# A Fourier mixing layer feeding a GEGLU block: a re-ordered opening, four weight scalings and one fold half moved to GpSimd, and new slots for the third batch's fold

## The chip, the cores and the metric

One core of one Trainium2 chip runs the whole program. The metric is the device time of one execution in microseconds (us); smaller is better. In what follows PE is TensorE, ACT is ScalarE, DVE is VectorE, POOL is GpSimd and SP is SyncE. PE multiplies, ACT and DVE empty PSUM, POOL works from SBUF alone, and SP only issues DMAs. POOL also issues DMAs: those that cast or gather.

## The reference

```
x: (8, 3008, 256) float32                      # batch, sequence, channels
a = real(fft(fft(x, axis=1), axis=2))          # mixing, float32
t = a.reshape(24064, 256)
g, v = t @ w_gate, t @ w_val                   # (256, 1536) each
out = (gelu(g) * v) @ w_out                    # exact gelu; (1536, 256)
```

## The kernel before

**The transform.** Each batch's sequence of 3008 is split as 94 x 32. The kernel first "folds" x: it adds and subtracts mirrored rows and channels, so that half-size transforms are left. `fold_ops` cuts this into five pieces of the 17 columns j: (13,4), (9,4), (5,4), (1,4), (0,1), each being start and count. A piece has a `first` (forward plus mirrored rows, lines 221 and 222) and a `second` (line 225). From batch 1 on there are two `combine` steps besides (line 229). The result is the tile `eo`. `s1` and `s1t` multiply it with the table G (lines 508 and 549), `ch` combines channels (line 530), and `tp_e`, `tp_o` and `tp_y` multiply with the table TP (lines 585, 590, 609). This leaves the even and odd halves E and O of one batch, and the row EB. The channel transform is not carried out on the data. `make_w` multiplies it into the gate and value weights instead (line 448): the table CW times the raw weights `w_raw` gives W for E, W for O, and "M", which is -2 times W for O except in row 0 (`keep2`, lines 463 and 465).

**The FFN.** A batch has three chunks of up to 512 token columns (512, 512, 481), each with twelve blocks of 128 hidden units. One block of one chunk is a **slot**: 36 slots for each batch, 288 in all. In slot i PE does the gate (`l1_gate`, E and O), then the mirrored gate of slot i-1 by adding M times O into the same PSUM bank (`l1_gate2`), then the value of this slot and of the one before. ACT applies gelu twice. DVE multiplies. POOL makes the mirrored half of h (line 732), except in the first eight slots, where the value too has three matmuls (`three`) and DVE does both halves (lines 707 and 724). The second layer (`l2_piece`, line 757) of a chunk runs in the slots of the next chunk.

**What sets the order.** Every engine runs its instructions in the order in which the program issues them; that order is written out by hand. `opening()` issues the loads, the tables and batch 0's transform, ending with E, O and the first 256 columns of W. `feed()` then walks the slots. In slot i it issues gate, gate2 of i-1, value, a piece of layer 2, then `pool[i]`, value2 of i-1, another piece of layer 2, and last `fill[i]`. `plan()` fills the two tables: `fill` holds what remains of the weights, batch 0's chunks 1 and 2, loads and transforms of later batches; `pool` holds the folds of batch b, by the list `slot_of`. The transform `s1t(b, jg, g)` of a piece stands no sooner than two slots after the slot of that piece's last fold step (`ready`). `load_part(b+1, k)` stands one slot after the `second` of the piece that frees its buffer.

**Loads in the opening.** SP loads columns 9 to 16 and 0 of batch 0 (`x_stage`). POOL issues 21 DMAs, in this order: five for batch 0 (`cast_mirror`, `cast_forward`), two each for w_raw columns 0-255, 256-511, 512-1023 and 1024-1535 (gate, then value), six for batch 1, and `load_wo(0)`, `load_wo(1)` for the two halves of w_out. Further down this numbering is used: DMA 10 and 11 are w_raw 512-1023, DMA 12 and 13 are w_raw 1024-1535, DMA 14 and 15 bring the first fold piece of batch 1. On SP, `load_part(2, ...)` brings the forward half of batch 2 into `x_raw`. Its buffer is the one that holds batch 0's `xb[0]`, so it can start when the last fold of batch 0 has read that.

**Warm-up matmuls.** `warm(n)` issues n matmuls of 512 columns on a zero tile; nothing reads their result.

Of the kernel before, what the change touches and what calls it, by code (L numbers as in the profile page):

```python
# [11 lines left out]
AF = mybir.ActivationFunctionType  # L12
ALU = mybir.AluOpType
# [15 lines left out]
def kernel(  # L29
# [8 lines left out]
    nc = tc.nc  # L38
# [8 lines left out]
    NK = 24  # L47
# [216 lines left out]
    def reduced(d, r, f):  # L264
        nc.vector.tensor_scalar(r, f, MAGIC, None, op0=ALU.add)
        nc.vector.scalar_tensor_tensor(d, r, MAGIC, f, op0=ALU.subtract, op1=ALU.subtract)
# [97 lines left out]

    def cw_phases():
        nc.scalar.activation(cf[:, 0:128], row_c, AF.Copy, scale=col_n0)
        reduced(cd[:, 0:128], cr[:, 0:128], cf[:, 0:128])

    def cw_magnitude():
# [22 lines left out]
    def t_columns():  # L392
        ps = psum("v")
        for i in range(5):
            nc.tensor.matmul(ps[:, i : i + 1], par[:, i, :], one[:, int(i == 0) : int(i == 0) + 1], start=True, stop=True)  # L395
        nc.scalar.activation(parc, ps[:, 0:5], AF.Copy)

    def t_phases():
        k1 = _sub(row_t, [[1, K1]], 0)
        for i in range(2):  # L400
            nc.scalar.activation(
                tf[:, i * K1 : (i + 1) * K1], k1, AF.Identity, scale=parc[:, 0:1], bias=parc[:, 1 + i : 2 + i])

    def t_reduced():
        reduced(td[:, :], tr[:, :], tf[:, :])
# [33 lines left out]

    V3_TO = 1024  # L440

    def make_w(i, f0, n, parts=(0, 1), engine="A", m_at=None, tag="dft"):

        def run():
            ps = psum(tag)
            for k, part in enumerate(parts):
                for half in range(2):
                    nc.tensor.matmul(  # L448
                        ps[:, k * n : (k + 1) * n], CW[:, part, half, :], w_raw[:, i, half, f0 : f0 + n],
                        start=half == 0, stop=half == 1)  # L450
            m = n * len(parts)
            dst = _sub(W_sb, [[F, len(parts)], [1, n]], (2 * i + parts[0]) * F + f0)
            if engine == "A":
                nc.scalar.activation(dst, ps[:, :m], AF.Copy)
            else:
                nc.vector.tensor_copy(dst, ps[:, :m])  # L456
            if 1 in parts and (i == 0 or f0 < V3_TO):
                def minus():
                    if i and f0 == 0:
                        W["v", "M"] = work([128, V3_TO], BF16, "osb", 3, "w_minus")[:, :]  # L460
                    dst, src = W["gv"[i], "M"][:, f0 : f0 + n], ps[:, m - n : m]
                    if engine == "A":
                        nc.scalar.activation(dst, src, AF.Copy, scale=keep2)
                    else:
                        nc.vector.tensor_scalar(dst, src, keep2, None, op0=ALU.mult)

                if m_at is None:
                    minus()
                else:
                    m_at.append(minus)  # L470
        return run
# [44 lines left out]
                nc.vector.tensor_copy(dst, src)  # L516
        return run

    def ch(b, pp, engine="A"):

        def run():
            st = state(b)
            A = st["A"]
            if "Z" not in st:
                st["Z"] = Z_tile()
            ps = ps_any(b)
            for q in range(2):
                k = 2 * (2 * pp + q)
                for g in range(2):
                    nc.tensor.matmul(  # L530
                        ps[:, q * C : (q + 1) * C], _sub(A, [[1, 128]], g * NK * K1 + k * K1), II[:, g, :, :],
                        start=g == 0, stop=g == 1)
            dst = _sub(st["Z"], [[1, 512]], pp * 512)
            if engine == "A":
                nc.scalar.activation(dst, ps[:, :], AF.Copy)
            else:
                nc.vector.tensor_copy(dst, ps[:, :])
        return run

    def s1t(b, jg, half):  # L540
# [252 lines left out]
    def opening():  # L793
        stage[0] = stage_tile()
        xb[0] = xb_tile(0)
        for j0, nj, at in ((9, 8, 0), (0, 1, 8)):
            nc.sync.dma_start(
                out=_sub(stage[0], [[1, nj * C]], at * C),
                in_=ap_replace(x, ap=[[32 * C, NPX], [1, nj * C]], offset=x.offset + j0 * C))
        pool_consts()  # L800
        index_consts(0)
        cast_mirror(0, 9, 8)
        pool_consts2()
        cast_mirror(0, 5, 4)
        cast_forward(0, 1, 8)
        index_consts(1)
        cast_mirror(0, 0, 1)
        cast_mirror(0, 1, 4)
        for f0, n in ((0, 256), (256, 256), (512, 512), (1024, 512)):
            load_w(f0, n)  # L810
        xb[1] = xb_tile(1)
        cast_forward(1, 9, 8)
        cast_mirror(1, 9, 8)
        cast_forward(1, 0, 9)
        for j0, nj in ((5, 4), (1, 4), (0, 1)):
            cast_mirror(1, j0, nj)
        for q in range(2):
            load_wo(q)
        idle = gelu_tile()[:, 0, :]
        nc.vector.memset(one[:, 0:1], 1.0)  # L820
        sin_table()
        nc.vector.memset(idle, 0.0)

        def warm(n):

            ps = psum("o")
            for _ in range(n):
                nc.tensor.matmul(ps[:, :], idle[:, 0:128], idle[:, :], start=True, stop=True)  # L828

        def fold_piece(j0, nj):  # L830
            for f in fold_ops(0, j0, nj, nc.vector):
                f()

        vec_consts()
        vec_fills()
        warm(7)
        g_phases()
        t_columns()
        t_phases()
        g_rows(9, 7)  # L840
        t_reduced()
        vec_consts2()
        identities()
        cw_phases()
        g_ends()
        cw_magnitude()
        vec_fills2()
        g_rows(1, 8)
        t_sin()
        cw_sin()  # L850
        gelu_table()
        warm(6)
        fold_piece(9, 4)
        s1(0, 2, 0)()
        s1(0, 2, 1)()
        warm(8)
        fold_piece(13, 4)
        cw_rest()
        fold_piece(5, 4)
        s1(0, 1, 0)()  # L860
        s1(0, 1, 1)()
        warm(2)
        fold_piece(0, 1)
        s1(0, 3, 0)()
        s1(0, 3, 1)()
        fold_piece(1, 4)
        t_write()
        s1(0, 0, 0)()
        s1(0, 0, 1, "V")()
        minus = []  # L870
        make_w(0, 0, 256, m_at=minus, tag="o")()
        ch(0, 0)()
        ch(0, 1, "V")()
        make_w(1, 0, 256, m_at=minus, tag="g")()
        tp_e(0, 0, 0, "V", tag="v")()
        tp_e(0, 0, 1, "A", tag="v")()
        minus[0]()
        minus[1]()

    def behind_first_gate():  # L880
        tp_y(0, 0)()

    NS = NG * NFC

    def plan():
# [8 lines left out]
            e = "A" if gi == 1 else "V"  # L894
            early += [ch(0, 2 * gi), ch(0, 2 * gi + 1, e), tp_e(0, gi), tp_o(0, gi, e), tp_y(0, gi)]
        for s, f in (
                (0, make_w(0, 256, 256)), (0, make_w(1, 256, 256, engine="V")), 
                (1, make_w(1, 512, 512, (1,))), (2, make_w(0, 512, 512, (0,), "V")), 
                (3, make_w(0, 512, 512, (1,))), (3, make_w(1, 512, 512, (0,), "V")),
                (4, make_w(1, 1024, 512, (1,), "V")), (5, make_w(0, 1024, 512, (0,), "V")),   # L900
                (6, make_w(0, 1024, 512, (1,))), (6, make_yw()), (7, make_w(1, 1024, 512, (0,), "V"))):
            at(fill, s, f)
        for i, f in enumerate(early):
# [21 lines left out]
        for b in range(1, B):  # L925
# [2 lines left out]
            for j0, nj in PIECES:  # L928
                ops += fold_ops(b, j0, nj, nc.gpsimd)
            per = len(ops) // 5  # L930
            first, n = {2: (s0 - 10, 27), 3: (s0 - 19, 30)}.get(b, (s0 - 22, 32))
            slot_of = [first + i * n // len(ops) for i in range(len(ops))]
            if b == 1:
                slot_of = [4, 4, 5, 5, 6, 6, 7, 7, 8, 8, 9, 13, 13, 14, 15, 15, 16, 17, 17, 18]
            for s, f in zip(slot_of, ops):
# [24 lines left out]
    def feed():  # L960
# [11 lines left out]
        for i, (parts, fc) in enumerate(blocks):  # L972
            if fc == 0 and i:
                assert not pend
                pend = list(works[i // NFC - 1])
            two = sooner.pop(i, []) if i <= NFC + 2 else [pend.pop(0) for _ in range(2) if pend]
            parts["G"][fc]()
            if i == 0:
                behind_first_gate()
            if before:  # L980
                before[0]["g"][before[1]]()
            parts["V"][fc]()
            if len(two) == 2:
                two.pop(0)()
            for f in pool.pop(i, []):
                f()
            if before:
                before[0]["v"][before[1]]()
            if two:
                two.pop(0)()  # L990
            for f in fill.pop(i, []):
                f()
            before = parts, fc
# [38 lines left out]
```

## Time and profile before

| | us |
|---|---|
| median of 9 runs | 623.9 |
| lowest, highest | 622.69, 625.6 |
| the profiled execution, own time | 623.92 |
| its span in the profile | 621.9 |
| E and O ready, first gate matmul of slot 0 | 20.85 |
| first fold step of batch 1 on POOL | 32.65 |
| first gate matmul of slot 3, of slot 18 | 27.16, 59.38 |
| first gate matmul of slot 36 (batch 1) | 95.46 |
| last matmul group begins | 616.58 |

The profiled execution lies at the median; about 2 us of its time lie outside the span. A slot takes about 2 us from there on. Times in the text are from the span's start. The profile's views used below are: the page of totals; the chain of work that ended last, followed back from the end; the instructions of an engine in order of time, with what ended the idle time before each in square brackets; the list of waits; and the bytes moved by each DMA queue within a stretch. "Landing" is the end of a transfer, counted from its issue.

### The profile page before, as it was taken

The numbers are of one execution on the slowest core, as the hardware profiler recorded it, in microseconds if no ns is written. First come the engines' busy times: TensorE is split into PE (matmuls) and PEld (weight loads), VectorE is DVE, ScalarE is ACT, GpSimd is POOL, SyncE is SP. The second block draws the span as 40 slices with busy tenths as digits, with TensorE's granted clock in tenths as the row PEclk, the third lists the DMA queues.
The fourth block names the chain that finished last, engine by engine and source line by source line (L and its number), as shares of the span: only waits on it lengthen the run. The fifth ranks groups of instructions, "written<-read, shape, count | busy, mean of one in ns | idle before, by whom it ended". The sixth has DMA issues, their size and how long they took to land.

```text
span 621.9 us, 12788 instructions
## 1 busy us (share of the span) xinstructions
PE 612.3 (98%) x4229; PEld 407.3 (66%) x4229; DVE 576.7 (93%) x939; ACT 426.0 (69%) x827; POOL 504.8 (81%) x510
## 2 busy tenths in 40 slices
PE   8999999999999999999999999999999999999997
PEld 3456666666766666666666666666666666666666
DVE  7589998999999999999999999999999999999992
ACT  5878677767776677667766667667676667666661
POOL 8389899999997999879997899979987655555651
PEclk9999999999999999999999999999999999999999
DMA  9961736555463353631644335543122321221123
GB/s 177 233 97 27 206 93 158 113 143 143 121 152 94 103 137 87 179 108 41 170 119 122 106 81 134 137 106 93 49 64 68 93 72 46 66 52 40 42 52 82
DMA packets 52464, 65.40 MB, mean 105 GB/s; under 512 B 7627, under 2 KB 47276, under 8 KB 50002
## 3 DMA queue, kind: packets, MB, share of 16 engines
q1 hardware_dynamic: 45470, 49.03, 30.2%
q0 software_dynamic: 6608, 15.29, 11.5%
q8 instruction: 33, 0.54, 0.4%
q10 hardware_dynamic: 320, 0.26, 0.2%
q14 instruction: 33, 0.27, 0.2%
HBM read 39.65 MB, written 30.17 MB: 112 GB/s over the span
## 4 chain that ended last, share of the span: by engine, by line
PE 91%; POOL 2%; DVE 2%; DMA 2%; issue 2%; ACT 1%; SPq 0%; DVEq 0%; ACTq 0%; POOLq 0%
PE ps_o L757 37%; PE ps_g L668 28%; PE ps_v L668 19%; PE ps_dft L549 2%; PE ps_dft L585 1%; PE ps_o L828 1%; DMA out_dram<-out_sb 1%; POOL h_sb L732 1%; DMA EB_sb<-yrow 1%; POOL eo_sb L229 1%; PE ps_dft L448 0%; SPq L662 0%; PE ps_v L395 0%; ACT gelu_sb L684 0%; POOL ab_sb L222 0%
## 5 line engine op out<-in xcount | busy, mean ns | idle before, releaser
L732 POOL TENSOR_TENSOR h_sb<-gelu_sb,v_sb 128x512 bf16<-128x512 bf16 (+1 forms) x280 | 319.5, 1146 | 88.2 <-DVE v_sb L730 82.8
L757 PE MATMUL ps_o<-Wo_sb,h_sb 128*128 128x256 bf16 (+1 forms) x2232 | 334.5, 273 | 0.6 <-POOL h_sb L732 0.6
L757 PEld LDWEIGHTS <-h_sb 128*128 128x128 bf16 (+1 forms) x2304 | 228.7, 100 | 111.7 <-POOL h_sb L732 1.9
L684 ACT ACTIVATE gelu_sb<-ps_g 128x512 bf16<-128x512 f32 (+1 forms) x288 | 169.5, 589 | 98.7 <-PE ps_g L668 90.6
L712 DVE SCALAR_TENSOR_TENSOR ve_sb<-EB_sb,yw,ps_v 128x512 f32<-128x512 bf16 (+1 forms) x280 | 206.3, 737 | 21.5 <-PE ps_v L668 18.3
L668 PEld LDWEIGHTS <-W_sb 128*128 128x128 bf16 x1440 | 138.0, 98 | 80.8 <-issue 3.2
L728 DVE TENSOR_TENSOR h_sb<-gelu_sb,ps_v 128x512 bf16<-128x512 bf16 (+1 forms) x280 | 189.8, 678 | 1.1 <-ACT gelu_sb L693 0.7
L730 DVE SCALAR_TENSOR_TENSOR v_sb<-ve_sb,ps_v 128x512 f32<-128x512 f32 (+1 forms) x280 | 187.4, 669 | 0.0
L668 PE MATMUL ps_g<-O_sb,W_sb 128*128 128x512 bf16 (+1 forms) x576 | 168.9, 374 | 0.1
L693 ACT ACTIVATE gelu_sb<-ps_g 128x512 bf16<-128x512 f32 (+1 forms) x288 | 168.8, 586 | 0.0
L668 PE MATMUL ps_g<-E_sb,W_sb 128*128 128x512 bf16 (+1 forms) x288 | 108.0, 375 | 0.7 <-ACT gelu_sb L693 0.4
L668 PE MATMUL ps_v<-E_sb,W_sb 128*128 128x512 bf16 (+1 forms) x288 | 108.0, 375 | 0.6 <-DVE W_sb L456 0.5
L668 PE MATMUL ps_v<-O_sb,W_sb 128*128 128x512 bf16 (+1 forms) x288 | 108.0, 375 | 0.0
L777 ACT ACTIVATE out_sb<-ps_o 128x512 f32<-128x512 f32 x92 | 55.0, 598 | 35.0 <-PE ps_o L757 34.7
L229 POOL TENSOR_TENSOR eo_sb<-ab_sb 94x512 bf16<-94x512 f32 (+1 forms) x70 | 77.6, 1110 | 0.5
L552 ACT ACTIVATE S_sb<-ps_dft 96x512 bf16<-96x512 f32 x56 | 33.0, 590 | 19.1 <-PE ps_dft L549 19.1
L225 POOL TENSOR_TENSOR ab_sb<-x_raw,x_raw 94x508 f32<-94x508 f32 (+1 forms) x30 | 33.0, 1100 | 0.0
L222 POOL TENSOR_TENSOR ab_sb<-x_raw,x_raw 94x508 f32<-94x508 f32 (+1 forms) x30 | 32.9, 1098 | 0.0
L549 PE MATMUL ps_dft<-eo_sb,G 94*96 94x256 bf16 x119 | 22.3, 272 | 0.2 <-POOL eo_sb L229 0.2
L595 ACT ACTIVATE E_sb<-ps_dft 128x512 bf16<-128x512 f32 (+1 forms) x23 | 13.5, 588 | 8.7 <-PE ps_dft L585 8.7
L163 POOL DMA_INDIRECT x_raw<-in_x_dram,idx x18 | 17.0, 947 | 2.9 <-issue 1.3
L595 ACT ACTIVATE O_sb<-ps_dft 128x512 bf16<-128x512 f32 (+1 forms) x22 | 13.0, 589 | 7.3 <-PE ps_dft L585 6.7
(151 smaller groups left out, 208.5 us busy)
## 6 DMA issues: line engine op xcount, KB each, us to landing
out_dram<-out_sb SPq DMA_DIRECT2D x364, 64.0 KB
x_raw<-in_x_dram SPq DMA_DIRECT2D x10, 768.0 KB
Z_sb<-z SPq DMA_DIRECT2D x7, 768.0 KB
z<-S_sb SPq DMA_DIRECT2D x7, 576.0 KB
EB_sb<-yrow SPq DMA_DIRECT2D x6, 376.2 KB
z<-S_sb SPq DMA_DIRECT2D x7, 192.0 KB
x_raw<-in_x_dram SPq DMA_DIRECT2D x2, 640.0 KB
x_stage<-in_x_dram SPq DMA_DIRECT2D x1, 768.0 KB
```

Source lines behind the costliest of these rows:

```text
L225: eng.tensor_tensor(ab(1, 1, up), mir(1, up), fwd(255, down), op=ALU.add)
L229: eng.tensor_tensor(_sub(eo, [[C, nj], [1, 128]], j0 * C + g * 128), ab(0, 0, [[1, 128]]), ab(1, 0, [[1, 128]]), op=op)
L549: nc.tensor.matmul(ps[:96, q * C : (q + 1) * C], G[:, j, :], _sub(eo, [[1, C]], j * C), start=(j == js[0]), stop=(j == js[-1]))
L668: nc.tensor.matmul(ps[:, :n], W[nm, part][:, fs], src, start=start, stop=stop, **kw)
L684: nc.scalar.activation(gl[:, 0, :n], pg[:, :n], AF.Gelu)
L693: nc.scalar.activation(_sub(gl, [[-1, n]], TOK + n - 1), pg[:, :n], AF.Gelu)
L712: nc.vector.scalar_tensor_tensor(ve[:, :n], EB_bufs[b][:, c0 : c0 + n], yw[:, fc : fc + 1], pv[:, :n], op0=ALU.mult, op1=ALU.add)
L728: nc.vector.tensor_tensor(st["h"][:, fc, 0, :n], gl[:, 0, :n], pv[:, :n], op=ALU.mult)
L730: nc.vector.scalar_tensor_tensor(_sub(vv, [[-1, n]], n - 1), ve[:, :n], 2.0, pv[:, :n], op0=ALU.mult, op1=ALU.subtract)
L732: nc.gpsimd.tensor_tensor(st["h"][:, fc, 1, :n], gl[:, 1, :n], vv[:, :n], op=ALU.mult)
L757: nc.tensor.matmul(pso[:m, half], st["h"][:, fc, sign, h0 : h0 + m], Wo_sb[:, fc, :], start=(fc == 0 and not (first and sign)), stop=(fc = ...
L777: nc.scalar.activation(_sub(osb, [[1, 2 * C]], 0, part_num=m), pso[:m, :], AF.Copy)
```

## The change

The tables CW and II of the channel step are made while DVE would wait for the TP table's phases; TP's phases are moved behind them, and behind the first fold piece. `warm(7)`, `warm(6)` and `warm(2)` become one `warm(16)` at the start; `warm(8)` stays. The `second` of fold piece (13,4) is issued on POOL, between the loads of w_raw 0-255 and 256-511. `cw_rest` and `t_write` move further down DVE's order. `ch` is cut into quarters that alternate between ACT and DVE. `tp_e(0,0,0)` goes to ACT and `tp_e(0,0,1)` to DVE. Of the "M" weights, the one for the value columns 0-255 goes to DVE, and four go to POOL, which reads W for O from SBUF instead of PSUM. `load_wo(1)` leaves the opening for slot 3. `tp_y(0,0)` leaves slot 0 for slot 5. Batch 2's folds get a list of slots written out by hand; before, the formula gives 26, 27, 28, 30, 31, 32, 34, 35, 36, 38, 39, 40, 42, 43, 44, 46, 47, 48, 50, 51.

```diff
     def make_w(... m_engine=None ...)
-                    if engine == "A":
+                    if m_engine == "P":
+                        nc.gpsimd.tensor_scalar(dst, W["gv"[i], "O"][:, f0 : f0 + n], keep2, None, op0=ALU.mult)
+                    elif (m_engine or engine) == "A":
                         nc.scalar.activation(dst, src, AF.Copy, scale=keep2)
...
     def opening():
...
         cast_mirror(0, 1, 4)
-        for f0, n in ((0, 256), (256, 256), (512, 512), (1024, 512)):
+        load_w(0, 256)
+        pool_second = fold_ops(0, 13, 4, nc.gpsimd)[1]
+        pool_second()
+        for f0, n in ((256, 256), (512, 512), (1024, 512)):
             load_w(f0, n)
...
-        for q in range(2):
-            load_wo(q)
+        load_wo(0)
...
         vec_consts()
         vec_fills()
-        warm(7)
+        warm(16)
         g_phases()
-        t_columns()
-        t_phases()
+        columns = t_columns()
         g_rows(9, 7)
-        t_reduced()
         vec_consts2()
         identities()
+        vec_fills2()
         cw_phases()
+        cw_reduced()
         g_ends()
         cw_magnitude()
-        vec_fills2()
         g_rows(1, 8)
+        t_phases(columns)
+        cw_sin()
+        fold_piece(9, 4)
+        t_reduced()
         t_sin()
-        cw_sin()
         gelu_table()
-        warm(6)
-        fold_piece(9, 4)
         s1(0, 2, 0)()
         s1(0, 2, 1)()
         warm(8)
-        fold_piece(13, 4)
-        cw_rest()
+        fold_ops(0, 13, 4, nc.vector)[0]()
         fold_piece(5, 4)
         s1(0, 1, 0)()
         s1(0, 1, 1)()
-        warm(2)
         fold_piece(0, 1)
         s1(0, 3, 0)()
         s1(0, 3, 1)()
         fold_piece(1, 4)
-        t_write()
         s1(0, 0, 0)()
+        cw_rest()
         s1(0, 0, 1, "V")()
         minus = []
         make_w(0, 0, 256, m_at=minus, tag="o")()
-        ch(0, 0)()
-        ch(0, 1, "V")()
-        make_w(1, 0, 256, m_at=minus, tag="g")()
-        tp_e(0, 0, 0, "V", tag="v")()
-        tp_e(0, 0, 1, "A", tag="v")()
+        ch(0, 0, qs=(0,))()
+        t_write()
+        ch(0, 0, "V", qs=(1,))()
+        ch(0, 1, qs=(0,))()
+        ch(0, 1, "V", qs=(1,))()
+        make_w(1, 0, 256, m_at=minus, m_engine="V", tag="g")()
+        tp_e(0, 0, 0, "A", tag="v")()
+        tp_e(0, 0, 1, "V", tag="v")()
         minus[0]()
         minus[1]()
...
     def plan():
...
-                (0, make_w(0, 256, 256)), (0, make_w(1, 256, 256, engine="V")), 
-                (1, make_w(1, 512, 512, (1,))), (2, make_w(0, 512, 512, (0,), "V")), 
-                (3, make_w(0, 512, 512, (1,))), (3, make_w(1, 512, 512, (0,), "V")),
-                (4, make_w(1, 1024, 512, (1,), "V")), (5, make_w(0, 1024, 512, (0,), "V")), 
+                (0, make_w(0, 256, 256, m_engine="P")), (0, make_w(1, 256, 256, engine="V", m_engine="P")),
+                (1, make_w(1, 512, 512, (1,), m_engine="P")), (2, make_w(0, 512, 512, (0,), "V")),
+                (3, make_w(0, 512, 512, (1,), m_engine="P")), (3, lambda: load_wo(1)), (3, make_w(1, 512, 512, (0,), "V")),
+                (4, make_w(1, 1024, 512, (1,), "V")), (5, make_w(0, 1024, 512, (0,), "V")), (5, tp_y(0, 0)),
...
-            first, n = {2: (s0 - 10, 27), 3: (s0 - 19, 30)}.get(b, (s0 - 22, 32))
+            first, n = (s0 - 19, 30) if b == 3 else (s0 - 22, 32)
             slot_of = [first + i * n // len(ops) for i in range(len(ops))]
+            if b == 2:
+                slot_of = [26, 27, 28, 29, 30, 31, 32, 33, 37, 38, 39, 40, 42, 43, 44, 45, 49, 49, 50, 51]
...
     def feed():
...
             parts["G"][fc]()
-            if i == 0:
-                behind_first_gate()
```

`ch(b, pp, engine, qs)` evacuates only the halves q in `qs`, into the same place of Z. `t_columns` now returns its PSUM tile, and `t_phases` copies it out; `cw_reduced` is the DVE half of `cw_phases`.

More of the change, by code (lines that the diff above doesn't have):

```diff
@@ L366, in cw_phases, with cw_reduced @@
         nc.scalar.activation(cf[:, 0:128], row_c, AF.Copy, scale=col_n0)
+    def cw_reduced():
         reduced(cd[:, 0:128], cr[:, 0:128], cf[:, 0:128])
@@ L395, in t_columns, with t_phases @@
             nc.tensor.matmul(ps[:, i : i + 1], par[:, i, :], one[:, int(i == 0) : int(i == 0) + 1], start=True, stop=True)
+        return ps
+    def t_phases(ps):
         nc.scalar.activation(parc, ps[:, 0:5], AF.Copy)
-    def t_phases():
         k1 = _sub(row_t, [[1, K1]], 0)
@@ L440, with make_w @@
     V3_TO = 1024
-    def make_w(i, f0, n, parts=(0, 1), engine="A", m_at=None, tag="dft"):
+    def make_w(i, f0, n, parts=(0, 1), engine="A", m_at=None, m_engine=None, tag="dft"):
         def run():
@@ L517, in s1, with ch @@
         return run
-    def ch(b, pp, engine="A"):
+    def ch(b, pp, engine="A", qs=(0, 1)):
         def run():
@@ L526, in run @@
             ps = ps_any(b)
-            for q in range(2):
+            for i, q in enumerate(qs):
                 k = 2 * (2 * pp + q)
@@ L530, in run @@
                     nc.tensor.matmul(
-                        ps[:, q * C : (q + 1) * C], _sub(A, [[1, 128]], g * NK * K1 + k * K1), II[:, g, :, :],
+                        ps[:, i * C : (i + 1) * C], _sub(A, [[1, 128]], g * NK * K1 + k * K1), II[:, g, :, :],
                         start=g == 0, stop=g == 1)
-            dst = _sub(st["Z"], [[1, 512]], pp * 512)
+            n = len(qs) * C
+            dst = _sub(st["Z"], [[1, n]], pp * 512 + qs[0] * C)
             if engine == "A":
-                nc.scalar.activation(dst, ps[:, :], AF.Copy)
+                nc.scalar.activation(dst, ps[:, :n], AF.Copy)
             else:
-                nc.vector.tensor_copy(dst, ps[:, :])
+                nc.vector.tensor_copy(dst, ps[:, :n])
         return run
@@ L816, in opening @@
             cast_mirror(1, j0, nj)
-        for q in range(2):
-            load_wo(q)
+        load_wo(0)
         idle = gelu_tile()[:, 0, :]
@@ L871, in opening @@
         make_w(0, 0, 256, m_at=minus, tag="o")()
-        ch(0, 0)()
-        ch(0, 1, "V")()
-        make_w(1, 0, 256, m_at=minus, tag="g")()
-        tp_e(0, 0, 0, "V", tag="v")()
-        tp_e(0, 0, 1, "A", tag="v")()
+        ch(0, 0, qs=(0,))()
[6 more added lines that the diff above has]
+        tp_e(0, 0, 1, "V", tag="v")()
         minus[0]()
         minus[1]()
-    def behind_first_gate():
-        tp_y(0, 0)()
     NS = NG * NFC
```

## The prediction, made before the result was known

> **What bounds the kernel now.** I first read the totals, then the engines' shares of the chain that ended last.
>
> ```profile
> PE 612.3 (98%) x4229; PEld 407.3 (66%) x4229; DVE 576.7 (93%) x939; ACT 426.0 (69%) x827; POOL 504.8 (81%) x510
> ...
> PE 91%; POOL 2%; DVE 2%; DMA 2%; issue 2%; ACT 1%; SPq 0%; DVEq 0%; ACTq 0%; POOLq 0%
> ```
>
> PE bounds nearly all of it. The change touches two stretches only, so I read the chain there. In the opening it runs through warm-up matmuls and table work until the first gate at 20.85:
>
> ```profile
> 11.77 3.41 PE ps_o L828 x8
> ...
> 16.64 1.26 ACT A_sb L514 x3
> ...
> 20.64 0.61 ACT O_sb L595
> ```
>
> The eight warm-ups take 3.41/8 = 0.427 us each and hold back the next fold products, whose data is ready. This is what the change can win. But I asked whether a gain there reaches the end, and read the chain on:
>
> ```profile
> 57.84 1.28 POOL eo_sb L229
> 59.12 0.04 issue
> 59.16 0.38 PE ps_dft L549 x2
> ```
>
> At 59.16 PE waits for POOL's fold of batch 1. POOL's own order of time shows where that began:
>
> ```profile
> 25.41 0.88 POOL L434 DMA_DIRECT2D Wo_sb<-in_moe_w_out_dram  x1 [4.82 <-DMA w_raw<-in_moe_w_gate_dram]
> 29.31 0.85 POOL L434 DMA_DIRECT2D Wo_sb<-in_moe_w_out_dram  x1 [3.02 <-DMA w_raw<-in_moe_w_val_dram]
> 32.65 0.21 POOL L221 TENSOR_TENSOR ab_sb<-xb 94x8 f32<-94x8 bf16 x1 [2.49 <-DMA xb<-in_x_dram,idx]
> ```
>
> POOL starts folding when the transfer lands, at 32.65, and is busy without a gap until 59.12. So PE can't pass 59.16 sooner than that transfer plus 26.5 us of POOL work, whatever the opening does. The first two lines matter as well: each w_out load waits for the w_raw transfer issued eight POOL DMAs before it (the 20th for the 12th, the 21st for the 13th), though it uses none of its data. Until now nothing stood behind them. Last, the waits of PE after 60 us: one of size.
>
> ```profile
> 102.43 0.28 PE L757 MATMUL ps_o<-Wo_sb,h_sb 128*128 128x256 bf16 x1 [0.64 <-POOL h_sb L732]
> ```
>
> **What the Trainium skill says.** "TensorE: Matmul & The Clock Gate", Part 1: PE starts at half rate and goes to full rate after a free-running window of about 3.4 us of sustained work; the trace agrees, warm-ups are 0.43 us apart until about 15 us and half that afterwards. "DMA: Bandwidth & Descriptors", Queues, rings and completion order: each DMA engine alternates between queues packet by packet. The trace agrees: while batch 2's x_raw loads on SP's queue, from 19 to 26 us, nearly equal packets move very unequal bytes:
>
> ```profile
> q1 hardware_dynamic: 223, 1.51, 83.7%
> q0 software_dynamic: 244, 0.24, 20.6%
> ```
>
> (packets, MB, share). "SBUF — State Buffer", SBUF: two separate sides: a DVE operation with two SBUF inputs and a POOL operation that reads SBUF exclude each other; no run here shows it.
>
> **Part by part.**
>
> *Warm-ups.* Sixteen at 0.427 are 6.83 us, from 1.24 to at most 8.07, two windows long, so one whole window is busy; the last eight then take 8 x 0.216 = 1.7 instead of 3.41, if the rate is kept. If it falls back in the gap before the fold, 1.7 us is lost again.
>
> *Tables and fold.* DVE idles 1.92 us before 7.77 and now makes II then (0.52 + 0.49). Fold (9,4) can start when its mirrored half lands, 1.91 + 7.0 = 8.9, not at 9.85. TP's phases cost ACT 0.18 + 0.78 after 9.1, so t_reduced waits to 10.1 and sits ahead of the later folds on DVE. Then landings bind: (5,4) at 4.84 + 7.1 = 11.9, (1,4) at 7.68 + 5.4 = 13.1. Fold (1,4) lasts 0.83 and ends near 14.1, against 15.28. ACT's seven evacuations, 0.37 apart after the gelu table at 12.5, end at 15.3. Quartered `ch` (0.4 for each half instead of 0.6 and 0.69), make_w and tp follow as before. E and O stand at about 18.3 and 18.7: the first gate is **2.6 us sooner** than 20.85.
>
> *Fold half on POOL.* A row of the same shape takes 1.14. It starts at 10.2, when DVE folds with two SBUF inputs. Free of charge for DVE at best; at worst, by the page above, DVE stands still 1.1 us and the later folds with it, so fold (1,4) ends at 15.0 and the gate gains 1.3. The later loads are issued 1.2 us later, which costs nothing while the DMA engines have a backlog, as they have from 2 to 38 us.
>
> *SP's queue.* SP starts x_raw when the last read of xb[0] ends (15.28; SP waited for that DVE line). Its packets moved from 19.0. With the fold ending at 14.1 they move from 17.8, while DMA 11 (12.23 + 6.7 = 18.9) is still under way. Then 11 takes the place that 12 has now and 12 that of 13, all 1.2 us sooner. Now 12 lands at 12.94 + 12.2 = 25.1 and 13 at 13.65 + 15.4 = 29.05; so 11 would land at 24, and **12 at about 29.05 - 1.2 = 27.9 instead of 25.1**. With DVE held up by POOL, x_raw is hardly sooner and 12 lands at 25.1 to 26.
>
> *M weights on POOL.* They leave 0.51, 0.68 and 0.68 us of ACT and 0.47 of DVE. On POOL no row shows the operation. From the two-input rows, 0.42 at 127 and 1.14 at 508 elements, it is at most 0.66 for 256 and 1.15 for 512; "GPSIMD Engine Reference", 3.1 gives 0.77 for 512 one-input elements at best, so about 0.4 for 256. I take 0.55 and 0.95. What counts is the queue: the first two stand **behind load_wo(0), which waits for DMA 12**. Done at: DMA 12 + 0.2 + 0.88 + 0.55. Gate2 of slot 2, in slot 3, needs it; it ran at 27.6. With 12 at 25.1 it is there at 26.8; with 26, at 27.7; with 27.9, at 29.6, that is 2.0 late, and everything behind it on PE too. A gate that is 2.6 us sooner just waits longer there.
>
> *load_wo(1) in slot 3.* Its M weight follows ACT's copy (29.69 before), so it is issued at 30.9 and ends by 31.8, ahead of 32.65: nothing, unless slot 3 is late by over 0.9. tp_y: 0.22 of PE moved from slot 0 to slot 5, nothing in sum unless slot 3 was pinned; 0.22 then.
>
> *Batch 2's folds.* Without folds in slots 34 to 36 the wait of 0.64 at 102.43 goes. But eight now stand in eight slots, and the transform of piece (9,4) moves with `ready` from slot 37 to slot 35. POOL begins slot 26's fold at 77.96 as before; behind it come two `first` (1.41 each), six more steps (1.22), seven h (1.07) and the gather of load_part (1.1): 77.96 + 2.8 + 7.3 + 7.5 + 1.1 = 96.7. PE reaches the end of slot 35 at 95.46. A new wait of **1.2 us** in place of 0.64: +0.6. If POOL keeps up with that, -0.64; if it lags a step more, +1.8.
>
> **Sum.** Up to 59.16: 0, since POOL's start is a landing and the bytes before it are unchanged. Slots 35 to 38: +0.6. The profiled 623.92 (at the median, 623.9) becomes **624.5**.
>
> **Rivals.** *A: the above*, 624.5, own range 623.9 to 625.3. *B: POOL's queue pins slot 3.* Price: slot 3 late by 2.0, + 0.22 for tp_y, less the 0.36 that PE lost at 59.16 (it was free at 58.80): +1.9, + 0.6 = 626.4. It decides from DMA 12 landing at about 26.3 on. For it: the order of the code, and the two waits of 4.82 and 3.02. Against it: DMA 12 lands in time if x_raw is not sooner. *C: the folds are swallowed*, POOL keeps up at slot 35 and the 0.64 is won: 623.3. For it: POOL idled 0.66 just before 77.96; against it, the sum above. *D: the opening's gain gets through*, because batch 1's input lands sooner or POOL needs less: 623.9 - 2.6 = 621.3, or 621.9 with +0.6. Against it: the DMA engines are full until 38 us and POOL has no gap. *That the warm-up doesn't do what it says* (rate falls back before the fold) loses 1.7 of the 2.6 and ends in A all the same.
>
> **How the numbers follow.** A 0.42, B 0.32, C 0.16, D 0.10. About 0.2% (1.25 us) is what a measurement of this kernel can tell from no change: faster is below 622.65, slower above 625.15. Faster: nearly all of D and a little of C, 0.11. Slower: five sixths of B and a quarter of A, 0.37. Same: 0.52. Range: 622.9 leaves out D, 626.6 the upper part of B. A and C share "no change", whose own range is 623.0 to 625.2.
>
> **What would show it.** Gate of slot 0 near 18.3 to 19.5; POOL's first fold of batch 1 still near 32.7, and PE again waiting for eo at about 59; a wait of PE for POOL's M weight in slot 3; x_raw issued near 14 or near 15; no PE wait at slot 38, one before slot 36. I am wrong if POOL folds before 31.5, or if slot 18 begins before 58.

## The result and the profile after

The changed kernel takes **627.98 us** (median of 10 runs, 624.89 to 630.55); the kernel before, 623.67 (31 runs). The ratio is 1.0068, 95% interval 1.0055 to 1.0080: slower by 4.3 us. The forecast was 624.5, range 622.9 to 626.6. The ten runs are spread wider than those of before (622.69 to 625.60). The profiled execution of after took 628.76, with a span of 627.0, that is 5.1 more than the span before.

First the totals and the engines' shares of the chain that ended last, after:

```profile
PE 611.6 (98%) x4230; PEld 406.7 (65%) x4230; DVE 578.5 (92%) x939; ACT 424.4 (68%) x824; POOL 510.9 (81%) x515
...
PE 91%; DMA 4%; POOL 2%; issue 1%; DVE 1%; ACT 0%; SPq 0%; ACTq 0%; POOLq 0%; DVEq 0%
```

PE's busy time is the same (612.3 before). What has grown on the chain is DMA, from 2% to 4%. Where that is, the chain shows in order of time. In the opening it no longer runs through warm-ups and ACT, but through one transfer and then POOL (the lines of `xb L163` and `Wo_sb L437` are loads that POOL issues):

```profile
13.48 13.14 DMA w_raw<-in_moe_w_val_dram
26.62 0.26 issue
26.88 0.90 POOL xb L163
...
29.98 0.88 POOL Wo_sb L437
30.86 0.03 issue
30.89 0.95 POOL W_sb L466
31.84 0.91 POOL w_minus L466
32.75 0.05 issue
32.79 0.39 PE ps_v L674
```

The transfer is DMA 11 (value columns 512-1023). It took 6.7 us before and takes 13.1 now. PE needs it in slot 1. PE in order of time, with the wait in brackets:

```profile
26.67 1.03 PE L451 MATMUL ps_dft<-w_raw,CW 128*128 128x512 bf16 x2 [4.24 <-DMA w_raw<-in_moe_w_val_dram]
```

POOL in order of time shows a second delay that begins with the same transfers. These lines answer to the three of POOL before:

```profile
29.98 0.88 POOL L437 DMA_DIRECT2D Wo_sb<-in_moe_w_out_dram  x1 [2.19 <-DMA w_raw<-in_moe_w_gate_dram]
30.89 0.95 POOL L466 TENSOR_SCALAR W_sb<-W_sb,keep 128x256 bf16<-128x256 bf16 x1
31.82 2.45 POOL L466 TENSOR_SCALAR w_minus<-W_sb,keep 128x256 bf16<-128x256 bf16 x2
34.34 1.56 POOL L466 TENSOR_SCALAR W_sb<-W_sb,keep 128x512 bf16<-128x512 bf16 x1
35.85 0.91 POOL L437 DMA_DIRECT2D Wo_sb<-in_moe_w_out_dram  x1
36.78 0.24 POOL L221 TENSOR_TENSOR ab_sb<-xb 94x8 f32<-94x8 bf16 x1
```

load_wo(0), the 20th DMA of POOL, waits for DMA 12 until 29.98. (The 19th, the last load of batch 1, had waited for DMA 11 in the same way, 6.36 us, until 26.88.) Behind load_wo(0) stand four M weights, 4.96 us together, and load_wo(1). Only then does POOL fold: at 36.78 instead of 32.65. PE reaches the transform that needs these folds (59.16 before) at 63.37, and the folds are done just before, so PE's own path and POOL's arrive together. Last, the wait at batch 2's folds. There is one before slot 36, and the one of 0.64 at slot 38 is gone:

```profile
101.01 0.38 PE L555 MATMUL ps_dft<-eo_sb,G 94*96 94x256 bf16 x2 [1.18 <-POOL eo_sb L229]
```

| gate of slot | 0 | 1 | 2 | 3 | 4 | 18 | 72 |
|---|---|---|---|---|---|---|---|
| before | 20.85 | 23.03 | 24.83 | 27.16 | 29.32 | 59.38 | 170.45 |
| after | 19.00 | 20.97 | 27.50 | 30.91 | 33.88 | 63.59 | 175.17 |
| difference | -1.85 | -2.06 | +2.67 | +3.75 | +4.56 | +4.21 | +4.72 |

Nearly the whole loss is made between slots 1 and 4, and 0.5 about slot 36. The first gate is sooner, as intended, but not by the warm-ups: the eight that held back the fold products before (3.41 us) still take 3.10.

### The profile page after: what moved, and what is told of

It reads as the page before. It is cut to its first block, busy times and chain, and to the rows that moved or that the text cites. A ratio compares the mean times of both kernels' runs of the same rounds, so it can differ in the third digit from the quotient of the medians.

```text
span 627.0 us, 12791 instructions
## 1 busy us (share of the span) xinstructions
PE 611.6 (98%) x4230; PEld 406.7 (65%) x4230; DVE 578.5 (92%) x939; ACT 424.4 (68%) x824; POOL 510.9 (81%) x515
## 4 chain that ended last, share of the span: by engine, by line
PE 91%; DMA 4%; POOL 2%; issue 1%; DVE 1%; ACT 0%; SPq 0%; ACTq 0%; POOLq 0%; DVEq 0%
PE ps_o L763 38%; PE ps_g L674 29%; PE ps_v L674 19%; PE ps_dft L555 2%; DMA w_raw<-in_moe_w_val_dram 2%; PE ps_dft L591 2%; DMA out_dram<-out_sb 1%; DMA x_stage<-in_x_dram 1%; POOL w_raw L431 1%; POOL xb L163 0%; PE ps_dft L451 0%; DVE v_sb L736 0%; PE ps_dft L535 0%; POOL eo_sb L229 0%; POOL eo_sb L225 0%
## 5 line engine op out<-in xcount | busy, mean ns | idle before, releaser
L718 DVE SCALAR_TENSOR_TENSOR ve_sb<-EB_sb,yw,ps_v 128x512 f32<-128x512 bf16 (+1 forms) x280 | 206.3, 737 | 21.3 <-PE ps_v L674 18.9
L163 POOL DMA_INDIRECT x_raw<-in_x_dram,idx x18 | 17.2, 953 | 2.9 <-issue 1.4
```

What stands on the lines that cost most here:

```text
L718: nc.vector.scalar_tensor_tensor(ve[:, :n], EB_bufs[b][:, c0 : c0 + n], yw[:, fc : fc + 1], pv[:, :n], op0=ALU.mult, op1=ALU.add)
```

## Experiments

Theory T: x_raw, which now starts right behind w_raw, takes the DMA engines from it; DMA 11 and 12 land late; PE waits, and POOL's M weights wait behind load_wo(0). Rivals: Q, the place and length of the M weights in POOL's queue would cost this whatever lands when; L, the fold half on POOL held back the issue of the loads; H, a start of x_raw that is 1.5 us sooner or later does not matter. Times are medians; the time that follows "against" is that of the kernel before on the same chip. The changed kernel's 627.98 is from the measurement above. What was expected stands ahead of each result, as it was put down before the run.

### x_raw out of the way, in both kernels

```diff
+    def hold():                       # hold_dram: one new row in DRAM
+        nc.sync.dma_start(out=hold_dram[:, :], in_=yw[0:1, :])
...
+        at(fill, 7, hold)
         for k, s in ((0, 8), (1, 9), (2, 9)):
             at(fill, s, lambda k=k: load_part(2, k, (load_forward,)))
```

The changed kernel with it:

> The changed kernel with one edit: batch 2's x_raw on SP's queue is held back to slot 7 (about 36 us) by a small transfer that reads yw. Theory T (x_raw's sooner start takes the DMA engines from w_raw, so DMA 11 lands at 26.6 instead of 18.9, and the rest follows): DMA 11 lands before 20.5 and DMA 12 before 22, PE's wait of 4.2 in slot 1 is gone, the clock stays full from 15 us on, POOL folds batch 1 from at most 33, and the time falls by 3 to 5, to 623 to 625. Rival Q (POOL's queue of M weights behind load_wo pins slots 3 and the fold, whatever lands when): the first fold stays above 35 and the time above 626.5. Rival L (the fold half on POOL held back the issue of the w_raw loads): DMA 11 still lands after 23, PE still waits over 2 us.

Measured: **622.17** against 623.72, ratio 0.9970 (0.9960 to 0.9981); 5.8 less than the changed kernel, more than the 3 to 5 that T had given. PE's wait in slot 1 is gone and slot 2 begins at 22.86. From 19 to 26 us the queues carried (packets, MB, share), after and then this run:

```profile
q1 hardware_dynamic: 267, 1.37, 79.0%
q0 software_dynamic: 293, 0.29, 24.8%
```

```profile
q0 software_dynamic: 763, 1.48, 112.5%
```

The engines are about equally full. But in after 79% of their time went to x_raw, which nobody needs before 78 us, and POOL's queue moved a fifth of the bytes it moves alone. With x_raw held, PE waits for none of POOL's M weights. POOL in order of time, in this run:

```profile
22.77 0.98 POOL L466 TENSOR_SCALAR W_sb<-W_sb,keep 128x256 bf16<-128x256 bf16 x1
23.70 2.48 POOL L466 TENSOR_SCALAR w_minus<-W_sb,keep 128x256 bf16<-128x256 bf16 x2
27.26 1.56 POOL L466 TENSOR_SCALAR W_sb<-W_sb,keep 128x512 bf16<-128x512 bf16 x1 [1.09 <-ACT W_sb L457]
28.77 0.91 POOL L437 DMA_DIRECT2D Wo_sb<-in_moe_w_out_dram  x1
29.70 0.24 POOL L221 TENSOR_TENSOR ab_sb<-xb 94x8 f32<-94x8 bf16 x1
```

The same 5 us of work end before the kernel before began to fold. T holds, and Q falls as the full cause. The control, the kernel before with the same hold, twice:

> Control: the same hold on the kernel before. DMA 12 then lands well before 25.1 and the six loads of batch 1 too, so POOL may fold from 29 to 31 instead of 32.65. Theory T, together with the forecast's reading that POOL's start sets slot 18: the wait for eo at 59 shrinks from 0.36 to nothing, so 623.1 to 623.7, no more, since PE is then free at 58.80 only. Rival Q: nothing moves, 623.7 plus or minus 0.3.

> The kernel before with x_raw held to slot 7, once more, beside the three above on the same chip: 621.5 to 622.2, to tell what the changed opening is worth when POOL's folds no longer stand behind x_raw. If the opening's gain of the forecast (2.6) were real for a kernel that isn't held at slot 18, the filled kernels would lie about 1.5 to 2.6 below this one; if the old opening has the same gate time whenever its clock rises early (19.03 was seen), they lie at most 1 below.

Measured: 621.73 (before 623.72; ratio 0.9963, 0.9949 to 0.9977), and on another chip 622.57 (before 623.96; 0.9977, 0.9966 to 0.9987). POOL folds from 25.90, sooner than the 29 to 31 that I expected, and the gain is 1.4 to 2.0 and not 0.6: my figure took PE to be free at 58.80, which was true of one execution only. The section on one part alone shows why. On the first chip both kernels ran with the hold: 622.17 with the change, 621.73 without it. With x_raw out of the way the change costs 0.4, about what the new slot list costs alone (0.35, below). So most of the 4.3 us comes of the change and x_raw together.

### One part undone at a time

The four M weights back on ACT and DVE (`m_engine="P"` struck out):

> The changed kernel with the four M weights back on ACT and DVE, x_raw as in it. Theory T: DMA 11 still lands at 26 to 27 and PE waits about 4 us for it in slot 1; what goes is the POOL work in front of the first fold (0.95 + 2.45 + 1.56 us) and PE's wait for w_minus at 32.8, so the fold starts at the landing near 34 instead of 36.8, and the time is 626 to 627. Rival Q (the queue is what costs): fold at 33, slot 3 near 28, 623.5 to 624.5.

Measured: 625.49 against 623.72, ratio 1.0025 (1.0015 to 1.0034). That is below the 626 to 627 of T and above the 623.5 to 624.5 of Q. In its profile DMA 11 happened to land in time: PE did not wait for it, and its one wait for w_raw is 0.32 us, for DMA 13. DMA 12 did not land in time, and the fold stood at the landing of batch 1's input, 33.54 (POOL, in order of time):

```profile
29.05 1.85 POOL L437 DMA_DIRECT2D Wo_sb<-in_moe_w_out_dram  x2 [7.02 <-DMA w_raw<-in_moe_w_gate_dram]
33.54 0.21 POOL L221 TENSOR_TENSOR ab_sb<-xb 94x8 f32<-94x8 bf16 x1 [2.64 <-DMA xb<-in_x_dram,idx]
```

So 2.5 of the 4.3 us go with the M weights in POOL's queue, given that DMA 12 is late. (DMA 11 was in time here and not in the profile of after; the next run, with DMA 11 in time and the M weights on POOL, is 2.1 above this one.) Q is half right: the queue does cost, but only because its head waits.

The fold half back on DVE:

> The changed kernel with the second half of fold (13,4) back on DVE. It takes the 1.2 us in which POOL issued nothing out of the load queue, and DVE's standstill with it. Theory T: fold (1,4) ends no later than in the changed kernel (14.4), x_raw starts at 17 to 17.5 as there, DMA 11 is delayed nearly as much and lands after 23; 626.5 to 628. Rival L (the late issue let the DMA engines run dry and put the w_raw loads behind x_raw): DMA 11 is issued 1.2 us sooner, has its bytes moved before x_raw begins, lands before 21, no PE wait over 1 us in slot 1, 624 to 625.

Measured: 627.58 against 623.72, ratio 1.0061 (1.0045 to 1.0078), about that of the changed kernel (four runs). DMA 11 landed by 21.7 and PE did not wait for it, as L had said and T had not. But PE met the other delay instead, the very one that the forecast's rival B described, and the time is the one that T had given:

```profile
29.59 0.61 PE L674 MATMUL ps_g<-O_sb,W_sb 128*128 128x512 bf16 x1 [4.08 <-POOL W_sb L466]
```

Which of the two PE meets depends on a landing that varies; in these two profiles both cost four us. As a full cause, L falls.

load_wo(0) moved behind the M weights:

```diff
-        load_wo(0)
         idle = gelu_tile()[:, 0, :]
...
-(3, lambda: load_wo(1)),
+(3, lambda: load_wo(0)), (3, lambda: load_wo(1)),
```

> The changed kernel with load_wo(0) moved from the opening to slot 3, behind the M weight there and next to load_wo(1), so that no M weight stands behind the load that waits for DMA 12. x_raw as in the changed kernel. If the forecast's step is right that the place in POOL's queue behind load_wo(0) is what makes the M weights late: the first M weights are done before 24, no PE wait for W or w_minus in slots 2 and 3, first fold at the landing of batch 1's first piece or right behind load_wo (33 to 35), 625 to 626, as with the M weights on ACT and DVE (625.5). If DMA 11's landing is what costs: PE still waits 3 to 4 us in slot 1, 627 to 628. If POOL's 5 us of M work are what costs, wherever they stand: fold still at 36 or later, 627 to 628.

Measured: 625.53 against 623.68, ratio 1.0037 (1.0022 to 1.0051), as much as taking the M weights off POOL. DMA 11 landed in time here too. The M weights of slots 0 and 1 now run at 24.25 to 27.96, the fold starts at the landing of batch 1's input, 33.78, and PE waits for it as the kernel before did:

```profile
60.29 0.38 PE L555 MATMUL ps_dft<-eo_sb,G 94*96 94x256 bf16 x2 [0.44 <-POOL eo_sb L229]
```

60.29 - 33.78 = 26.51. The forecast's rule "fold start plus 26.5" holds.

x_raw held only until TP is written. It was meant to start as late as before, but was issued at 17.79, 2.5 us later than there (the edit is against x_raw_late):

```diff
-        nc.sync.dma_start(out=hold_dram[:, :], in_=yw[0:1, :])
+        nc.sync.dma_start(out=hold_dram[:, :], in_=TP[0:1, 0, 0, :])
```

> The changed kernel with x_raw held back on SP only until DVE has written the table TP (about 16.3 us), so that its packets start at 19 to 19.5, as they did in the kernel before, instead of 17.5. Theory T (the sooner start is what hurts): DMA 11 lands before 22 and PE has no wait over 1 us for it in slot 1; DMA 12 lands at 25 to 27 as before; what stays is POOL's M weights behind load_wo(0), so PE may wait 1 to 2 us in slots 2 to 3; 624.5 to 626. Rival H (the hold to 36 us helped because x_raw was out of the way altogether, and its start 1.5 us sooner or later hardly matters): DMA 11 lands after 24 or DMA 12 after 28, 627 to 628.

Measured: 625.56 against 623.68, ratio 1.0031 (1.0021 to 1.0041). DMA 11 and 12 land in time: POOL issues load_wo(0) at 22.18 without waiting, and there is no PE wait in slots 1 to 3. The time is in T's range, and H falls. But the end stays 1.9 above the kernel before, because now batch 1's input lands late and the fold stands at it. That x_raw's bytes, only moved along, delay it is the likely reading; no run isolates it:

```profile
35.04 0.21 POOL L221 TENSOR_TENSOR ab_sb<-xb 94x8 f32<-94x8 bf16 x1 [4.60 <-DMA xb<-in_x_dram,idx]
```

Put side by side, one number goes with DMA 12's landing: how long before x_raw it is issued, its head start. The last column is the time at which load_wo(0), which waits for that landing, runs. (wo_late is not in the table, since no load_wo waits there; with a head start of 0.95 the last of DMA 12's 16 parts landed at 28.2.)

| run | x_raw issued | DMA 12 issued | head start | load_wo(0) runs at |
|---|---|---|---|---|
| after | 14.51 | 14.19 | 0.32 | 29.98 |
| m_back | 14.79 | 14.47 | 0.32 | 29.05 |
| opening_alone | 14.89 | 14.57 | 0.32 | 27.78 |
| fold_back | 13.92 | 12.95 | 0.97 | 27.68 |
| slots_alone | 14.08 | 12.95 | 1.13 | 26.87 |
| before | 15.31 | 12.94 | 2.37 | 25.41 |
| x_raw_as_before | 17.79 | 14.65 | 3.14 | 22.18, no wait |

Of the 2.05 us of head start that after lost, 1.25 are the later issue (L has that part) and 0.80 the sooner x_raw. Seven profiles that differ in other things too go together with the head start; they do not prove it to be the only cause.

### One part alone

The opening alone: M weights, load_wo(1) and slot list as before.

> The changed kernel with the M weights back on ACT and DVE, load_wo(1) back in the opening, and batch 2's folds in their old slots: what is left of the change is the opening (and tp_y in slot 5). The forecast said of this part: nothing, 623.9, since POOL's first fold is a landing at 32.65. Theory T, after what was seen with the M weights back (fold at the landing 33.5, i.e. 0.9 later, 625.5, of which the slot list is 0.5): fold at 33 to 34, slot 18 at 26.5 + 0.4 us behind it, 624.5 to 625.2. If the opening's gain got through: 621.5 to 622.5.

Measured: 625.27 against 623.96, ratio 1.0026 (1.0014 to 1.0039). The time is 0.07 above what was expected, the way there is another: the fold starts at 32.51, as before, and this time PE's path is the late one. It waits 2.15 us for DMA 11 in slot 1:

```profile
25.52 0.59 PE L451 MATMUL ps_dft<-w_raw,CW 128*128 128x512 bf16 x2 [2.15 <-DMA w_raw<-in_moe_w_val_dram]
```

Then it takes 5.57 us from slot 2 to slot 4, against 4.49 before; the clock was at half from 26.8 to 30.2. The gate of slot 0 was 0.9 sooner than before; slot 18 began 2.0 later.

The slot list alone, in the kernel before:

> The kernel before with the change's slot list for batch 2's folds and nothing else. The forecast's term: a wait of 1.2 at slot 35 in place of the 0.64 at slot 38, +0.6, 624.2 to 624.5. If the list pays: 623.1 to 623.4.

Measured: 624.16 against 623.81, ratio 1.0008 (1.0000 to 1.0016): +0.35, at the edge of what can be told. In the profile it is +0.5 from slot 18 to slot 72 (111.57 against 111.07), with a wait of 1.2 us for eo. This run, with the old opening, shows something else. First the eight warm-ups of before, then this run's, with its first gate, its first fold and the transform that needs it:

```profile
11.57 3.61 PE L828 MATMUL ps_o<-gelu_sb 128*128 128x512 bf16 x8
```

```profile
10.43 1.89 PE L828 MATMUL ps_o<-gelu_sb 128*128 128x512 bf16 x8
...
18.12 0.38 PE L668 MATMUL ps_g<-E_sb,W_sb 128*128 128x512 bf16 x1 [0.24 <-DVE E_sb L597]
```

```profile
32.12 0.21 POOL L221 TENSOR_TENSOR ab_sb<-xb 94x8 f32<-94x8 bf16 x1 [2.38 <-DMA xb<-in_x_dram,idx]
```

```profile
58.61 0.04 issue
58.65 0.38 PE ps_dft L549 x2
```

The old opening has its warm-ups at full clock here, and its first gate at 18.12: 2.73 sooner than in the profile that I had read, and sooner than in after. Slot 18 is 0.51 sooner (58.87). So first, the opening of the kernel before already has what the change was to win, in some executions. And second, what the opening wins is swallowed at slot 18, where PE waits for the fold: 32.12 + 26.53 = 58.65. With x_raw held the fold is sooner and the swallowing ends. The runs of before_x_raw_late_again with a mean clock of 1.0 took 620.76 to 623.61, median 621.6, those with 0.999 took 623.15 to 624.68, median 623.6, while for the kernel before, beside them, the medians of the two groups are 624.1 and 623.8. The profile with the early clock (slots_alone) has a mean of 1.0 and the one with the late clock (before) 0.999; that this holds for the other runs, and so that an early clock pays once x_raw is held, is likely but not shown.

### Towards a better kernel

All with x_raw held to slot 7. First batch 2's old slots, and a list with the eighth step in slot 34:

> x_raw held to slot 7, and batch 2's folds in the slots of the kernel before. Against the same with the new list (622.17) the wait of 1.2 at slot 35 goes and the one of 0.64 at slot 38 comes back: 0.5 to 0.6 less, 621.6. If the slot list costs nothing once POOL is ahead: 622.0 to 622.4.

> x_raw held to slot 7, and a list of my own for batch 2's folds: the eighth step in slot 34 instead of 33, the rest as in the change, so that the transform of piece (9,4) stands in slot 36 instead of 35. POOL should end the eighth step before PE comes there: no wait of 1.2 at slot 35 and none of 0.64 at slot 38: 620.9 to 621.2. If POOL's backlog only moves on, a wait of 0.6 to 1.2 shows at slots 36 to 38 and the time is 621.6 to 622.2.

Measured, on the same chip: 623.31 (621.34 to 624.31; ratio 0.9988, 0.9979 to 0.9997) and 623.14 (621.46 to 625.15; ratio 0.9984, 0.9974 to 0.9994). Both miss; x_raw_late had given 622.17 on another chip. Each has two levels, 621.5 and 623.7. By the profiles, from slot 18 to slot 72, the new list takes 111.58, the old one 111.09 and mine 111.22: the new list costs 0.5, and mine wins nothing. The levels come from ahead of that: the first gate is at 19.31 in one profile and at 21.37 in the other. Two causes were open, a clock that falls back in PE's gap ahead of the first fold products, and DVE held up by POOL's fold half. Three runs take the first edit below alone, both, and the second alone; the fourth repeats both. All have x_raw held and batch 2's old slots.

```diff
         columns = t_columns()
+        warm(8)
...
-        pool_second = fold_ops(0, 13, 4, nc.gpsimd)[1]
-        pool_second()
...
-        fold_ops(0, 13, 4, nc.vector)[0]()
+        fold_piece(13, 4)
```

> x_raw held to slot 7, batch 2's old slots, and eight warm-up matmuls more behind t_columns, where PE otherwise idles 2.3 us ahead of the first fold products. If the two levels of the same kernel without them (about 621.5 and 623.8) come from the clock falling back in that gap: slot 0 at 18.0 to 19.0, clock full from the first rise on, times in one group of 620.5 to 621.5. If they come from DVE being held up by POOL's fold half (PE waits 1.05 us for the second half of fold (9,4) in some executions and 0.25 in others): still two levels, and slot 0 above 20 in the upper one.

> The same with the second half of fold (13,4) on DVE again. If POOL's fold half holds DVE up: the wait of 1.05 to 1.2 us for fold (9,4) is never there, w_raw's loads are issued 1.2 to 1.5 us sooner, and the time is 0.5 to 1 below the filled kernel with the half on POOL, in one group, 620 to 621. If the half on POOL is worth its place: equal or 0.3 slower.

> x_raw held to slot 7, batch 2's old slots, the second half of fold (13,4) on DVE, no filler. If DVE's standstill beside POOL makes the upper level: one group near 621 to 621.7, no wait over 0.3 us between the two halves of fold (9,4). If the clock does: two levels as before, 621 and 623, median above 621.8.

> The filled kernel with the fold half on DVE again, with more rounds: 620.8 to 621.6, that is 2.2 to 3 below the kernel before.

Measured: the filler alone 622.53 (621.68 to 624.24; before 623.96), still two levels. Both 621.23 (before 623.96; the slowest of its four runs, 622.85, waited 1.1 us for batch 2's row besides), and on another chip **620.82** (620.51 to 620.95) against 623.81, ratio 0.9954 (0.9940 to 0.9968). The fold half on DVE without the filler, beside it, **620.77** (620.47 to 621.71), ratio 0.9955 (0.9943 to 0.9968). So the half on POOL made the upper level. The profiles of all runs agree: with the half on POOL, DVE's fold (9,4) took 3.2 to 3.3 us in the three profiles whose first gate came at 21.3 to 21.4 (wo_late, late_slots_36, late_old_slots_filled), and 2.2 to 2.3 in the six with a gate at 19.0 to 19.9. With the half on DVE it took 1.3. With it back on DVE the filler buys nothing that the time shows, though the first gate moved from 19.21 to 17.84 in the profiles. These versions beat the kernel before by 2.7 to 3.0 us and the changed one by about 7. But the kernel before wins 1.4 to 2.0 of that by the hold alone. On the chip where both were measured, the version with the filler alone is level with it (622.53 against 622.57) and the one with both edits 1.3 below. These versions keep the change's M weights on POOL, for which PE does not wait once w_raw lands in time.

## Why the prediction was wrong, step by step

**The step that failed** is "Up to 59.16: 0, since POOL's start is a landing and the bytes before it are unchanged". POOL's start was 36.78 and not a landing; it was POOL's queue. The rule around it was right in every run held there: 26.5 us from the first fold to the transform. Three terms under it were wrong:

1. *"The later loads are issued 1.2 us later, which costs nothing while the DMA engines have a backlog".* A backlog says that the engines stay full, not whose bytes they move. The head start over x_raw fell from 2.37 to 0.32 us. So w_raw's last three loads came under x_raw's bytes, and load_wo(0), at the head of POOL's queue, waited. The prediction had worked out a late DMA 12 itself, 27.9, but its sum took the other case, in which DVE's standstill beside POOL keeps x_raw from being sooner. DVE did stand still, and x_raw was sooner all the same: the last fold ended at 14.44, not at 15.0.
2. *The M weights' price and their last reader.* I took 0.55 and 0.95 for 256 and 512 columns and judged them by gate2 of slot 2, which runs in slot 3. They measured 0.95 and 1.56, above even the upper bounds of 0.66 and 1.15 that I had drawn from the two-input rows. And what they delayed for longest was the fold behind them. I had also written "nothing, unless slot 3 is late by over 0.9" for load_wo(1); slot 3 was late by 3.75. Rival B had the mechanism and its condition, DMA 12 after 26.3 (it was 29.7), but its 626.4 priced slot 3 alone and left the fold behind it out. m_back and wo_late put this point at 2.5 of the 4.3 us.
3. *DMA 11.* I had worked out that it would land at 24 and asked only what that does to DMA 12. Its own reader, in slot 1, came up at 22.4 in after; the opening as forecast would have had it there sooner still. In after PE waited 4.24, in opening_alone 2.15. In both the clock fell as well, which no term held. opening_alone puts the opening, this wait in it, at 1.3.

**What was right, and what was luck.** That x_raw would move sooner with the fold and delay w_raw came true. The first gate came within 18.3 to 19.5 (19.00), but not on the way forecast: 1.85 sooner and not 2.6, with the eight warm-ups at 3.10 and not 1.7, since the rate had fallen back, which the prediction had allowed for. The new wait before slot 36: 1.2 forecast, 1.18 found; net 0.6 forecast, 0.5 in the profiles, 0.35 in the medians. That the opening's gain would not reach the end: slots_alone shows it, by accident. Rival D fell for the same reason, and C with slot 36. Rival D's price was wrong besides: the trace of before was one execution with a late clock, so "2.6 us sooner" compared a change with a chance.

**What stays open.** DMA 11 lands at about 20 in some executions and at 26 in others. In after, 14 of its 16 parts had landed by 20.5, the last two at 25.0 and 26.6; in opening_alone two came at 25.2 and 25.4. DMA 12 has such a straggler even before: 15 parts by 21.8, the last at 25.1. Why one or two parts lag, and not the others, no run told. Nor does a run tell how much of after's 4.3 belongs to each of points 2 and 3, since PE meets now one, now the other.

## What to carry to other kernels

A step that issues DMAs later, or frees a buffer sooner, changes the order of bytes even when the engines are full; for each transfer that moves, look for its own first reader and not only for the one in your theory. Work put on a queue is priced behind the head of that queue, and its cost is read at what is next there. Before counting a gain at an early mark, look whether the same kernel already shows it in another execution, and what pins the time later on.

## What the runs showed of the hardware

*The clock can fall with an idle stretch of PE and stay down when work is back.* Stretches of after (time, length, then PE's busy time and number, PEld, DVE, ACT, POOL, the granted clock, the DMA share and GB/s):

```profile
19.90:23.40 3.50, 2.53 (x16) 1.36 (x14) 2.39 (x4) 2.25 (x4) 0.62 (x1) 1.00 1.07 241
23.40:26.80 3.40, 0.13 (x1) 0.13 (x2) 0.21 (x1) 0.00 (x0) 0.00 (x0) 0.70 1.09 226
26.80:30.20 3.40, 3.40 (x9) 1.20 (x8) 0.25 (x1) 1.68 (x3) 1.12 (x2) 0.50 1.13 218
30.20:33.60 3.40, 3.28 (x12) 0.94 (x11) 2.42 (x5) 1.08 (x2) 3.37 (x4) 0.79 1.04 207
```

PE is fully busy from 26.8 on, and the granted clock is still at half until 31.6. In opening_alone the wait of 2.15 us ended at 25.5 and the clock fell after it, from 26.8 to 30.2. So a wait costs more than its length; there the surcharge was 5.57 - 4.49 = 1.1 us.

*DVE and POOL.* The prediction cited the Trainium skill's "SBUF — State Buffer", SBUF: two separate sides, for their mutual exclusion and had no run for it. Now there are some. DVE's second half of fold (9,4), in after, where POOL's half of fold (13,4) stands at 10.14, and in fold_back, where that half is not on POOL:

```profile
8.73 1.63 DVE L225 TENSOR_TENSOR eo_sb<-xb,x_stage 94x508 bf16<-94x508 bf16 x1
```

```profile
8.99 0.67 DVE L225 TENSOR_TENSOR eo_sb<-xb,x_stage 94x508 bf16<-94x508 bf16 x1
```

All nine profiles with the half on POOL have at least one such operation of DVE that is about 1 us longer, and no profile without it has one. POOL's half takes 1.20 to 1.68 us; POOL's rows of this shape for batch 1 take 1.14. So the two disturb each other. That one waits for the whole instruction of the other, as the page says, is not shown: in after DVE's operation would have been over at 9.41 at its usual length, before POOL's is recorded to begin.

*POOL's scalings.* The Trainium skill's "GPSIMD Engine Reference", 3.1 led me to 0.77 us at best for 512 elements. A scaling of 128x512 bf16 elements by one number for each partition measured 1.56 to 1.57 in every run that has it on POOL; for 256, 0.91 to 0.98. That is longer than POOL's two-input row of 508 elements, 1.14. The measurement decides.
